# Two gated linear-attention blocks: x and A's k weights chunk by chunk over two queues, and block 2's transposing transfers over two queues

## The chip, the cores and the metric

The kernel runs on one core of a Trainium2 chip. The metric is the device time of one execution in microseconds; three executions of the kernel before are shown, and their median counts.

## The reference

One input x (2048 rows of 640, bf16) goes through two linear-attention blocks A and B, each with its own weights, and a gate mixes the two results row by row. B_x is not used.

```python
def _A_ref(x, wqkv, wo):                      # _B_ref is the same
    B, S, D = x.shape                         # 1, 2048, 640
    H = 32; Dh = D // H                       # 32 heads of 20
    qkv = ((x @ wqkv).reshape(B, S, 3, H, Dh)).transpose(2, 0, 3, 1, 4)
    q, k, v = qkv[0], qkv[1], qkv[2]
    phi = lambda t: jnp.where(t > 0, t + 1, jnp.exp(t)) + 1e-6
    pq, pk = phi(q), phi(k)
    kv = jnp.einsum("bhsd,bhse->bhde", pk, v)
    z = jnp.einsum("bhsd->bhd", pk)
    num = jnp.einsum("bhqd,bhde->bhqe", pq, kv)
    den = jnp.einsum("bhqd,bhd->bhq", pq, z)[..., None] + 1e-6
    return (num / den).transpose(0, 2, 1, 3).reshape(B, S, D) @ wo

g = sigmoid((x * gate_w).sum(-1, keepdims=True))
return g * _A_ref(x, A_wqkv, A_wo) + (1 - g) * _B_ref(x, B_wqkv, B_wo)
```

## The kernel before

The rows are cut into 16 chunks of 128 (index i) and 4 blocks of 512 (index n; block 1 holds chunks 0 to 3, block 2 chunks 4 to 7). The 640 columns are cut into 5 pieces of 128 (index c). TensorE needs x with its columns on the partitions, as the tile xT. Block 1 gets there by TensorE itself: x is loaded as it stands into xn, each chunk is transposed into PSUM (`x_transpose`, L167 to L172) and copied to xT by VectorE or ScalarE. Blocks 2 to 4 are brought by transposing transfers, one for each piece c of a block, from x in memory straight into xT (L105 to L112).

The work that the change touches lies at the start:

- L99 to L104 issue the first loads. SP's queue carries x chunks 0 and 1 in one transfer, A's k weights of pieces 1 and 3, and x chunks 2 and 3. ScalarE's queue carries A's k weights of pieces 0, 2 and 4, and the row of gate weights (`grow`), which `gate_columns` (L139) reads late in A's k stage.
- L105 to L112 issue the transposing transfers, all on SP's queue: five for block 2, then A's q weights in one transfer, then five each for blocks 3 and 4. Later loads (x for the g pass L487, A's v and output weights L437 to L445) follow on the same queue.
- L115 to L132 build masks and the identity on POOL, and L135 to L137 run eight matmuls on zeros.
- `k_first` (L197 to L210) is the first stage that reads x. It transposes chunks 0 and 1 and then runs their k matmuls with c as the outer loop, so that both chunks use each piece of the weights as it comes; chunks 2 and 3 are transposed before chunk 1's last two matmuls.
- `k_chunk` (L190 to L195) does one chunk of k: ten matmuls (two halves of 320 columns, five pieces each) into a PSUM slot, and then `k_done`, which is `phi` (L174 to L179): one exponential on ScalarE and two operations on VectorE, which write the feature map pk.

There are four PSUM slots (`ps`, L56 to L65), taken in turn; a slot is free again when `phi` or the copy has read it. After `k_first` the program runs k chunks 2 to 7 (L478), five q units of the first two blocks (L480), k chunks 8 to 15 (L482), and then the later stages: q, the sums z, the g pass (x against pk), the products with v and the output weights, then the same for B, and at last the output rows in pairs.

Nothing in this part fixes the order of the work by hand. The framework takes the program's order as a priority, may move an instruction ahead of one that is not ready by its plan, and writes each engine's instructions out in one fixed order; it also puts in every wait. Only the last stage (from L526) has an order written by hand.

Of the kernel before, what the change touches and what calls it, by code (L numbers as in the profile page):

```python
# [8 lines left out]
P = 128  # L9
FP32 = mybir.dt.float32  # L10
BF16 = mybir.dt.bfloat16
ACT = mybir.ActivationFunctionType
ALU = mybir.AluOpType

S, D, H = 2048, 640, 32
Dh = D // H
DT = D // P
ST = S // P
NB = 4
CB = 4  # L20
HB = 512
# [9 lines left out]
def kernel(  # L31
# [11 lines left out]
    nc = tc.nc  # L43
    x2 = A_x.flatten_outer_dims()
# [4 lines left out]
    wpool = ctx.enter_context(tc.tile_pool(name="wpool", bufs=1))  # L49
    work = ctx.enter_context(tc.tile_pool(name="work", bufs=2))  # L50
# [5 lines left out]
    def ps_raw(name, slot=None):  # L56

        if slot is None:
            slot = turn[0]
            turn[0] = (slot + 1) % 4  # L60
        return psum.tile([P, 4 * HB], BF16, tag=f"ps{slot}", name=name)

    def ps(name, slot=None):

        return ps_raw(name, slot).bitcast(FP32).rearrange("p (b n) -> p b n", b=2)  # L65

    xT = persist.tile([P, DT, S], BF16, name="xT")
    xn = persist.tile([P, ST, D], BF16, name="xn")
# [12 lines left out]
    zero = persist.tile([P, HB], BF16, name="zero")  # L81
    grow = persist.tile([1, D], BF16, name="grow")
# [4 lines left out]
    wq_dram = [A_wqkv.rearrange("(c p) f -> p c f", p=P), B_wqkv.rearrange("(c p) f -> p c f", p=P)]  # L87
# [6 lines left out]
    xb0 = x2[0:CB * P, :].rearrange("(p q) d -> p q d", q=CB)  # L94
    wk = [None, None]
    wv = [None, None]
    wq = [None, None]
    wk[0] = wpool.tile([P, DT, D], BF16, tag="wk", name="wkA")
    nc.sync.dma_start(out=xn[:, 0:2, :], in_=xb0[:, 0:2, :])  # L99
    for c in range(DT):  # L100
        eng = nc.sync if c % 2 else nc.scalar
        eng.dma_start(out=wk[0][:, c, :], in_=wq_dram[0][:, c, D:2 * D])
    nc.sync.dma_start(out=xn[:, 2:4, :], in_=xb0[:, 2:4, :])
    nc.scalar.dma_start(out=grow[:], in_=gate_w.rearrange("(o f) -> o f", o=1))  # L104
    for n in range(1, NB):  # L105
        if n == 2:
            wq[0] = wpool.tile([P, DT, D], BF16, tag="wq", name="wqA")
            nc.sync.dma_start(out=wq[0][:], in_=wq_dram[0][:, :, 0:D])
        for c in range(DT):
            nc.sync.dma_start_transpose(  # L110
                out=xT[:, c, n * HB:(n + 1) * HB], in_=x2[n * HB:(n + 1) * HB, c * P:(c + 1) * P]
            )  # L112


    make_identity(nc, ident[:])  # L115
# [4 lines left out]
    for sign, base in ((1, 0), (-1, Dh - 1)):  # L120
        nc.gpsimd.affine_select(
            out=maskE[:], in_=maskE[:], pattern=[[sign * P, DT], [-sign * Dh, H]],
# [3 lines left out]
    for r in range(4):  # L126
        rows = slice(32 * r, 32 * r + 32)
        for sign, base in ((1, 0), (-1, Dh - 1)):
            nc.gpsimd.affine_select(
                out=E4[rows], in_=E4[rows], pattern=[[sign, D]],  # L130
# [2 lines left out]


    warm = ps("warm", 3)  # L135
    for k in range(8):
        nc.tensor.matmul(warm[:, 0, :], lhsT=zero[:, 0:P], rhs=zero[:], start=True, stop=True)  # L137

    def gate_columns():  # L139
# [24 lines left out]
            nc.scalar.activation(out=ge[b][:], in_=pt[:, 0, :], func=ACT.Exp, scale=(-1.0, 1.0)[b])  # L164
            nc.vector.tensor_scalar(ge[b][:], ge[b][:], 1.0, 1e30, op0=ALU.add, op1=ALU.min)

    def x_transpose(i, slot, eng):  # L167
        pt = ps_raw("xt", slot)
        for c in range(DT):
            nc.tensor.transpose(out=pt[:, c * P:(c + 1) * P], in_=xn[:, i, c * P:(c + 1) * P], identity=ident[:])  # L170
        copy = nc.scalar.copy if eng == "act" else nc.vector.tensor_copy
        copy(out=xT[:, :, i * P:(i + 1) * P], in_=pt[:, 0:D].rearrange("p (c n) -> p c n", c=DT))  # L172

    def phi(dst, src, n):  # L174

        e = work.tile([P, 2, n], BF16, tag="e", name="e", bufs=3)
        nc.scalar.activation(out=e[:], in_=src, func=ACT.Exp)  # L177
        nc.vector.tensor_scalar(e[:], e[:], 1.0, EPS, op0=ALU.min, op1=ALU.add)  # L178
        nc.vector.scalar_tensor_tensor(out=dst, in0=src, scalar=1.0 + EPS, in1=e[:], op0=ALU.add, op1=ALU.max)  # L179

    def k_mm(b, i, c, pt, hf):
        nc.tensor.matmul(  # L182
            pt[:, hf, 0:HF], lhsT=xT[:, c, i * P:(i + 1) * P], rhs=wk[b][:, c, hf * HF:(hf + 1) * HF],
            start=(c == 0), stop=(c == DT - 1),
        )

    def k_done(b, i, pt):
        phi(pk[:, i, :].rearrange("p (b n) -> p b n", b=2), pt[:, :, 0:HF], HF)

    def k_chunk(b, i):  # L190
        pt = ps(f"k{'AB'[b]}")
        for hf in range(2):
            for c in range(DT):
                k_mm(b, i, c, pt, hf)
        k_done(b, i, pt)  # L195

    def k_first():  # L197

        x_transpose(0, 0, "dve")
        x_transpose(1, 1, "act")  # L200
        pts = [ps("kA", 2 + i) for i in range(2)]
        for c in range(DT):
            for i in range(2):
                for hf in range(2):
                    k_mm(0, i, c, pts[i], hf)
                if c == DT - 1 and i == 0:
                    x_transpose(2, 0, "dve")
                    x_transpose(3, 1, "act")
        for i in range(2):
            k_done(0, i, pts[i])  # L210

    def q_unit(b, m, h):

# [260 lines left out]


    k_first()
    turn[0] = 0
    for i in range(2, ST // 2):  # L478
        k_chunk(0, i)
    for m in range(DT):  # L480
        q_unit(0, m, 0)
    for i in range(ST // 2, ST):  # L482
        if i == ST - 1:
            gate_columns()
        k_chunk(0, i)
    for n in range(1, NB):
        nc.sync.dma_start(  # L487
            out=xn[:, n * CB:(n + 1) * CB, :], in_=x2[n * HB:(n + 1) * HB, :].rearrange("(q p) d -> p q d", p=P)
# [10 lines left out]

    turn[0] = 2  # L500
    k_chunk(1, 0)
    k_chunk(1, 1)
    kvt_pass(0)
# [22 lines left out]
    with tc.manual_schedule():  # L526
# [23 lines left out]
        for i in range(1, half):  # L550
            p, after = pairs[i], pairs[i + 1] if i + 1 < half else None
# [42 lines left out]
```

## Time and profile before

| what | value |
|---|---|
| median of 3 executions | 202.93 us |
| the three executions | 202.90, 202.93 and 229.24 us |
| the profiled execution's own time | 203.25 us |
| its span, first to last instruction | 201.5 us |
| TensorE busy | 195.9 us, 97% of the span |
| VectorE busy | 140.1 us, 70% |
| ScalarE busy | 76.4 us, 38% |
| transfers, mean over the span | 71 GB/s, 14.21 MB |

The profile is of one execution. Its views give a start in us from the span's beginning, a length in us, then the engine, the line of the program, the operation and what it writes and reads; a letter q behind an engine's name (SPq, ACTq) means its queue, which issues transfers and waits. "x5" counts the instructions that a row merges. PE is TensorE, DVE VectorE, ACT ScalarE, SP SyncE. A matmul's own duration in a row is longer than its share of the time, since matmuls are pipelined; the distance between two starts is what counts. The view of waits names who waited, what for, the sum in us, how many times, and the longest.

### The profile page before, as it was taken

The numbers are of one execution on the slowest core, as the hardware profiler recorded it, in microseconds if no ns is written. First come the engines' busy times: TensorE is split into PE (matmuls) and PEld (weight loads), VectorE is DVE, ScalarE is ACT, GpSimd is POOL, SyncE is SP. The second block draws the span as 40 slices with busy tenths as digits, with TensorE's granted clock in tenths as the row PEclk, the third lists the DMA queues.
The fourth block names the chain that finished last, engine by engine and source line by source line (L and its number), as shares of the span: only waits on it lengthen the run. The fifth ranks groups of instructions, "written<-read, shape, count | busy, mean of one in ns | idle before, by whom it ended". The sixth has DMA issues, their size and how long they took to land.

```text
span 201.5 us, 3645 instructions
## 1 busy us (share of the span) xinstructions
PE 195.9 (97%) x1527; PEld 123.1 (61%) x1527; DVE 140.1 (70%) x224; ACT 76.4 (38%) x105; POOL 8.5 (4%) x22
## 2 busy tenths in 40 slices
PE   7999999999999999999999999999999999999992
PEld 3676457654566667877764444566667667777761
DVE  3288679857894577677678767876578667885552
ACT  2354545454413442356552454415442531122110
POOL 8800000000000000000000000000000000000000
PEclk9999999999999999999999999999999999999999
DMA  6679479950140000140052000000000002222111
GB/s 192 183 185 155 105 214 368 190 163 3 12 152 3 0 0 3 15 148 3 0 135 53 0 0 0 5 0 0 3 0 0 3 0 87 78 79 83 65 68 65
DMA packets 18016, 14.21 MB, mean 71 GB/s; under 512 B 8736, under 2 KB 17745, under 8 KB 18001
## 3 DMA queue, kind: packets, MB, share of 16 engines
q1 hardware_dynamic: 17566, 13.50, 25.3%
q10 hardware_dynamic: 434, 0.49, 0.7%
q8 instruction: 12, 0.20, 0.4%
q14 instruction: 4, 0.02, 0.0%
HBM read 9.40 MB, written 2.62 MB: 60 GB/s over the span
## 4 chain that ended last, share of the span: by engine, by line
PE 96%; ACT 1%; DVE 1%; issue 0%; ACTq 0%
PE gB L236 11%; PE gA L236 11%; PE kA L182 11%; PE qA L218 11%; PE kB L182 11%; PE qB L218 11%; PE oy L376 5%; PE ox L376 5%; PE oz L376 5%; PE ow L376 3%; PE warm L137 2%; PE mA L300 1%; PE mid L300 1%; PE exA L352 1%; PE exB L352 1%; PE mid L279 1%
## 5 line engine op out<-in xcount | busy, mean ns | idle before, releaser
L182 PEld LDWEIGHTS <-xT 128*128 128x128 bf16 x320 | 31.0, 98 | 12.9 <-DVE xT L172 0.7
L236 PEld LDWEIGHTS <-xn 128*128 128x128 bf16 x320 | 29.8, 98 | 14.1 <-issue 2.5
L178 DVE TENSOR_SCALAR e<-e 128x640 bf16<-128x640 bf16 (+1 forms) x52 | 19.0, 366 | 18.9 <-ACT e L177 17.4
L236 PE MATMUL gB<-pk,xn 128*128 128x320 bf16 x160 | 23.3, 300 | 0.0
L236 PE MATMUL gA<-pk,xn 128*128 128x320 bf16 x160 | 23.3, 300 | 0.0
L182 PE MATMUL kA<-wkA,xT 128*128 128x320 bf16 x160 | 22.9, 302 | 0.1
L182 PE MATMUL kB<-wkB,xT 128*128 128x320 bf16 x160 | 22.9, 299 | 0.0
L218 PE MATMUL qA<-xT,wqA 128*128 128x512 bf16 x100 | 22.2, 379 | 0.0
L218 PE MATMUL qB<-xT,wqB 128*128 128x512 bf16 x100 | 22.0, 379 | 0.0
L218 PEld LDWEIGHTS <-wqB 128*128 128x128 bf16 x100 | 9.6, 98 | 11.4 <-issue 0.3
L218 PEld LDWEIGHTS <-wqA 128*128 128x128 bf16 x100 | 9.5, 97 | 11.4 <-issue 0.3
L177 ACT ACTIVATE e<-kB 128x640 bf16<-128x640 f32 x16 | 11.3, 704 | 11.7 <-PE kB L182 11.7
L177 ACT ACTIVATE e<-kA 128x640 bf16<-128x640 f32 x16 | 11.3, 705 | 11.3 <-PE kA L182 11.3
L177 ACT ACTIVATE e<-qA 128x1024 bf16<-128x1024 f32 x10 | 10.2, 1023 | 13.1 <-PE qA L218 13.1
L177 ACT ACTIVATE e<-qB 128x1024 bf16<-128x1024 f32 x10 | 10.2, 1023 | 13.1 <-PE qB L218 13.1
L179 DVE SCALAR_TENSOR_TENSOR pk<-kB,e 128x640 bf16<-128x640 f32 x16 | 13.2, 824 | 1.6
L179 DVE SCALAR_TENSOR_TENSOR pk<-kA,e 128x640 bf16<-128x640 f32 x16 | 13.2, 824 | 1.5
L179 DVE SCALAR_TENSOR_TENSOR pqTB<-qB,e 128x1024 bf16<-128x1024 f32 x10 | 12.2, 1218 | 0.9
L179 DVE SCALAR_TENSOR_TENSOR pqTA<-qA,e 128x1024 bf16<-128x1024 f32 x10 | 12.2, 1218 | 0.9
L410 ACT COPY u<-ox 128x320 f32<-128x320 f32 x8 | 3.4, 425 | 21.4 <-PE ox L376 21.4
L365 DVE TENSOR_TENSOR pqTA<-exA,pqTA 128x1024 bf16<-128x1024 f32 (+1 forms) x6 | 6.3, 1046 | 5.8 <-PE exA L352 5.8
L365 DVE TENSOR_TENSOR pqTB<-exB,pqTB 128x1024 bf16<-128x1024 f32 (+1 forms) x6 | 6.3, 1046 | 5.8 <-PE exB L352 5.8
(90 smaller groups left out, 220.6 us busy)
## 6 DMA issues: line engine op xcount, KB each, us to landing
out_dram<-osb SPq DMA_DIRECT2D x15, 160.0 KB, 1.8
xn<-in_A_x_dram SPq DMA_DIRECT2D x3, 640.0 KB, 6.0
wqA<-in_A_wqkv_dram SPq DMA_DIRECT2D x1, 800.0 KB, 5.4
wvA<-in_A_wqkv_dram SPq DMA_DIRECT2D x1, 800.0 KB, 9.8
wkB<-in_B_wqkv_dram SPq DMA_DIRECT2D x1, 800.0 KB
wqB<-in_B_wqkv_dram SPq DMA_DIRECT2D x1, 800.0 KB, 4.6
wvB<-in_B_wqkv_dram SPq DMA_DIRECT2D x1, 800.0 KB, 4.6
woA<-in_A_wo_dram SPq DMA_DIRECT2D x1, 750.0 KB, 12.2
```

The costliest lines, as they stand in the source:

```text
L137: nc.tensor.matmul(warm[:, 0, :], lhsT=zero[:, 0:P], rhs=zero[:], start=True, stop=True)
L177: nc.scalar.activation(out=e[:], in_=src, func=ACT.Exp)
L178: nc.vector.tensor_scalar(e[:], e[:], 1.0, EPS, op0=ALU.min, op1=ALU.add)
L179: nc.vector.scalar_tensor_tensor(out=dst, in0=src, scalar=1.0 + EPS, in1=e[:], op0=ALU.add, op1=ALU.max)
L182: nc.tensor.matmul(pt[:, hf, 0:HF], lhsT=xT[:, c, i * P:(i + 1) * P], rhs=wk[b][:, c, hf * HF:(hf + 1) * HF], start=(c == 0), stop=(c == D ...
L218: nc.tensor.matmul(pt[:, u, :], lhsT=wq[b][:, c, m * P:(m + 1) * P], rhs=xT[:, c, n * HB:(n + 1) * HB], start=(c == 0), stop=(c == DT - 1),)
L236: nc.tensor.matmul(pt[:, hf, 0:HF], lhsT=xn[:, i, c * P:(c + 1) * P], rhs=pk[:, i, hf * HF:(hf + 1) * HF], start=(i == 0), stop=(i == ST - 1),
L300: nc.tensor.matmul(pt[:, hf, 0:HF], lhsT=KVT[:rows, j, c * P:(c + 1) * P], rhs=wo_sb[b][:rows, j, hf * HF:(hf + 1) * HF], start=(k == 0), ...
L352: nc.tensor.matmul(pts[j // 2][:, j % 2, k * RB:(k + 1) * RB], lhsT=E4[32 * j:32 * j + 32, m * P:(m + 1) * P], rhs=rT[32 * j:32 * j + 32, ...
L365: nc.vector.tensor_tensor(out=dst, in0=src, in1=dst, op=ALU.mult)
L376: nc.tensor.matmul(dst, lhsT=left[:, c, r0:r0 + P], rhs=right[:, c, :], start=(first and c == 0), stop=(c == DT - 1), skip_group_check=not ...
L410: nc.scalar.copy(out=self.u2[:], in_=self.at("x"))
```

## The change

The first x load is cut, so that x comes as chunk 0, chunk 1, and chunks 2 and 3. These and A's five k weight pieces go out alternately on SP's and ScalarE's queues; the gate row moves to POOL's queue. Block 2's five transposing transfers are issued in the order c = 0, 3, 1, 4, 2, with 3 and 4 from ScalarE's queue and the others from SP's. A's q weights come after them on SP's queue and before block 3, as they did. A one-element exponential on ScalarE (`first`) is put between the first loads and the transposing transfers. Six matmuls on zeros run for eight.

In `k_first`, chunk 0's copy to xT is made in two parts (pieces 0 and 1, then 2 to 4), chunk 1's copy moves from ScalarE to VectorE, and the k matmuls run chunk by chunk (`k_chunk`), each half with c inside it, no longer piece by piece over both chunks. Chunks 2 and 3 are transposed between chunk 1's two halves. Nothing that is computed changes.

```diff
-    nc.sync.dma_start(out=xn[:, 0:2, :], in_=xb0[:, 0:2, :])
-    for c in range(DT):
-        eng = nc.sync if c % 2 else nc.scalar
+    def load_x(eng, lo, hi):
+        eng.dma_start(out=xn[:, lo:hi, :], in_=xb0[:, lo:hi, :])
+
+    def load_wk(eng, c):
         eng.dma_start(out=wk[0][:, c, :], in_=wq_dram[0][:, c, D:2 * D])
-    nc.sync.dma_start(out=xn[:, 2:4, :], in_=xb0[:, 2:4, :])
-    nc.scalar.dma_start(out=grow[:], in_=gate_w.rearrange("(o f) -> o f", o=1))
-    for n in range(1, NB):
-        if n == 2:
-            wq[0] = wpool.tile([P, DT, D], BF16, tag="wq", name="wqA")
-            nc.sync.dma_start(out=wq[0][:], in_=wq_dram[0][:, :, 0:D])
+
+    def load_xT(eng, n, c):
+        eng.dma_start_transpose(
+            out=xT[:, c, n * HB:(n + 1) * HB], in_=x2[n * HB:(n + 1) * HB, c * P:(c + 1) * P]
+        )
+
+    load_x(nc.sync, 0, 1)
+    load_wk(nc.scalar, 0)
+    load_wk(nc.sync, 1)
+    load_x(nc.scalar, 1, 2)
+    load_wk(nc.scalar, 2)
+    load_wk(nc.sync, 3)
+    load_wk(nc.scalar, 4)
+    load_x(nc.sync, 2, 4)
+    first = work.tile([P, 1], BF16, tag="first", name="first", bufs=1)
+    nc.scalar.activation(out=first[:], in_=zero[:, 0:1], func=ACT.Exp)
+    nc.gpsimd.dma_start(out=grow[:], in_=gate_w.rearrange("(o f) -> o f", o=1))
+    for c, eng in ((0, nc.sync), (3, nc.scalar), (1, nc.sync), (4, nc.scalar), (2, nc.sync)):
+        load_xT(eng, 1, c)
+    wq[0] = wpool.tile([P, DT, D], BF16, tag="wq", name="wqA")
+    nc.sync.dma_start(out=wq[0][:], in_=wq_dram[0][:, :, 0:D])
+    for n in range(2, NB):
         for c in range(DT):
-            nc.sync.dma_start_transpose(
-                out=xT[:, c, n * HB:(n + 1) * HB], in_=x2[n * HB:(n + 1) * HB, c * P:(c + 1) * P]
-            )
+            load_xT(nc.sync, n, c)
...
-    for k in range(8):
+    for k in range(6):
         nc.tensor.matmul(warm[:, 0, :], lhsT=zero[:, 0:P], rhs=zero[:], start=True, stop=True)
...
-    def x_transpose(i, slot, eng):
+    def x_transpose(i, slot, eng, cuts=()):
...
-        copy(out=xT[:, :, i * P:(i + 1) * P], in_=pt[:, 0:D].rearrange("p (c n) -> p c n", c=DT))
+        src = pt[:, 0:D].rearrange("p (c n) -> p c n", c=DT)
+        for lo, hi in zip((0, *cuts), (*cuts, DT)):
+            copy(out=xT[:, lo:hi, i * P:(i + 1) * P], in_=src[:, lo:hi])
...
-    def k_chunk(b, i):
-        pt = ps(f"k{'AB'[b]}")
+    def k_chunk(b, i, slot=None, between=None):
+        pt = ps(f"k{'AB'[b]}", slot)
         for hf in range(2):
             for c in range(DT):
                 k_mm(b, i, c, pt, hf)
+            if hf == 0 and between is not None:
+                between()
         k_done(b, i, pt)
 
     def k_first():
 
-        x_transpose(0, 0, "dve")
-        x_transpose(1, 1, "act")
-        pts = [ps("kA", 2 + i) for i in range(2)]
-        for c in range(DT):
-            for i in range(2):
-                for hf in range(2):
-                    k_mm(0, i, c, pts[i], hf)
-                if c == DT - 1 and i == 0:
-                    x_transpose(2, 0, "dve")
-                    x_transpose(3, 1, "act")
-        for i in range(2):
-            k_done(0, i, pts[i])
+        x_transpose(0, 0, "dve", (2,))
+        x_transpose(1, 1, "dve")
+        k_chunk(0, 0, 2)
+        k_chunk(0, 1, 3, lambda: [x_transpose(2, 0, "dve"), x_transpose(3, 1, "act")])
```

## The prediction, written before the result was known

> **What bounds the kernel now.** I read the page's busy shares first, then the chain of work that ended last in order of time, then SP's and ScalarE's timelines, the waits of SP's queue, and the answer on the line that issues the transposing transfers (L110).
>
> ```profile
> PE 195.9 (97%) x1527; PEld 123.1 (61%) x1527; DVE 140.1 (70%) x224; ACT 76.4 (38%) x105; POOL 8.5 (4%) x22
> ```
>
> TensorE is busy for 97% of the span, so an edit pays only if TensorE starts sooner, or costs if TensorE is left without data. Both can only happen in the first 20 us, where the chain reads (start, length, what):
>
> ```profile
> 1.26 3.60 PE warm L137 x8
> 4.85 0.55 PE xt L170 x5
> ...
> 5.97 2.97 PE kA L182 x18
> 8.94 0.56 PE xt L170 x10
> 9.50 0.29 PE kA L182 x2
> ...
> 9.81 8.32 PE kA L182 x60
> 18.13 10.79 PE qA L218 x50
> ```
>
> Two things are to be seen. First, from 9.81 on TensorE runs without a pause: 60 matmuls in 8.32 us, 0.136 us apart, are chunks 2 to 7, ten matmuls and 1.36 us each. Chunk 4, the first that reads block 2 (rows 512 to 1023), starts at 9.81 + 2 x 1.36 = 12.53. Second, the start runs at half pace: five transposes take 0.55 us at 4.85, ten take 0.56 us at 8.94; 18 matmuls take 2.97 us where 18 x 0.136 = 2.45 would do. The half pace ends near 6.7 us, some 5.5 us after the first matmul, although the page's clock row reads full from its first slice.
>
> ```profile
> 4.66 6.41 SPq L110 DMA_TRANSPOSE xT<-in_A_x_dram  x5
> 11.12 0.58 SPq L108 DMA_DIRECT2D wqA<-in_A_wqkv_dram  x1
> 11.75 13.91 SPq L110 DMA_TRANSPOSE xT<-in_A_x_dram  x10
> ```
>
> SP needs 6.41 us to issue block 2's five transposing transfers, 1.26 to 1.30 us each. The last is issued at about 9.82.
>
> ```profile
> L110 SPq DMA_TRANSPOSE xT<-in_A_x_dram x5: 1210/1258/1259, 4.7 to 9.8; - x5
> ...
> DMA to landing us min/median/max: 2.8/2.9/3.5
> ```
>
> From issue to landing such a transfer takes 2.8 to 3.5 us (2.7 is the least over all 15), so the last one lands at about 9.82 + 3.1 = 12.9 and chunk 4 reads it at 12.53 + 4 x 0.136 = 13.07. Block 2 is 0.2 us early: the line that this change works on has almost no slack.
>
> ```profile
> SPq L110 <- DMA wkA<-in_A_wqkv_dram: 2.0, 1, 2.0
> ```
>
> The first transposing transfer stood 2.0 us on SP's queue until a part of A's k weights had landed, data that it does not read. The program's waits are the framework's, and it makes these transfers wait for transfers of the other queue.
>
> **The change part by part.**
>
> *Loads.* x comes as chunk 0, chunk 1 and chunks 2-3; SP still issues four transfers, ScalarE four (chunk 1 in place of the gate row). At 0.39 to 0.45 us each both queues end near 2.6 as now. The first x load now carries 160 KB for 320, which landed 3.7 us after its issue at 0.8, at 4.5; the bytes to wait for halve, so I put x chunk 0 at 3.6 (between 3.3 and 4.5). The gate row moves to POOL's queue; POOL has the identity ready at 1.54, wanted at 3.8, and the row's reader is at 38.4, so nothing. Two warming matmuls fewer: 3.60 / 8 x 2 = 0.9 us, used only because x comes earlier. The one-element exponential costs below the 0.70 us of the smallest one here, on a ScalarE idle until 5.96, and takes the 1.28 us table load with it; nothing. If that cover went, each would delay ScalarE's transfers by that much.
>
> *First k chunks.* The same 20 transposes and 20 matmuls run in another order. Chunk 0's copy in two pieces is 0.49 us plus one fixed cost (0 to 0.49) on an idle VectorE; chunk 1's copy moves from ScalarE (0.69) to VectorE (0.49), behind them. TensorE could begin at 3.85 instead of 4.64, 0.8 us sooner, but at half pace, and k weights c=3 and c=4 still land near 6. Chunks 2 and 3 of x are transposed in chunk 1's middle, and VectorE may be in chunk 0's 0.40 + 0.82 us when its copy is due. Chunk 2 would start between 9.1 and 9.9, for 9.81 now: a gain of 0.7 to a loss of 0.1.
>
> *Block 2's transfers.* The order issued is c0 SP, c3 ScalarE, c1 SP, c4 ScalarE, c2 SP. The trace has no two of them on different queues. The nearest rows are the two ends: issued side by side, they go out one per 1.26 us and queue; one after the other, each costs a whole landing of 2.7 to 3.1 us. I take the second, because of the 2.0 us wait above: these transfers are held until another queue's transfer has landed. The Trainium skill, "DMA: Bandwidth & Descriptors", section "Silent corruption: two transposing streams in flight at once", speaks against the change: the transfers of two issuing engines must not be in flight together, and the later stream waits for the earlier one's full completion. No run here shows it; by that page the sum is the one below, by side-by-side issue it would be 202.6.
>
> The chain then is c0, c3, c1, c4, c2: four changes of queue. c0 queues behind x chunks 2-3, which landed at 7.2; it landed at 8.1 itself. It may be issued earlier than 4.66 now, so it lands between 6.3 (3.6 + 2.7) and 8.2; I take 7.5. Four landings of 2.9 (2.7 to 3.1, with 0.05 for the wait) are 11.6 (11.0 to 12.6). c2 lands at 19.1 (17.3 to 20.8). Chunk 4 reads c2 as its third matmul, now at 12.53 + 0.27 = 12.80. **TensorE loses 19.1 - 12.8 = 6.3 us** (4.5 to 8.0), and the front's 0.7 vanishes in that stall.
>
> What stands behind the waits. On ScalarE, c4's transfer can only go at about 13.4 and holds the queue 1.26 us: x chunk 3's copy and the exponentials of chunks 0 to 2 come after it if they are queued behind it. That moves chunk 3 to about 16, still before 19.1, so it adds nothing; VectorE then has four chunks of 1.2 us behind, less than TensorE's next 1.36 each. On SP, A's q weights and blocks 3 and 4 stand behind c2. The weights go at about 17.5 and land 5.4 us later at 22.9; the first q matmul follows c2 by 5.2 us, at 24.3. The slack is 1.4 us as now, and blocks 3 and 4 shift with TensorE. If the weights slip more, TensorE waits for them next.
>
> *The clock.* TensorE will stand nearly idle for 5 to 6 us. The trace before has no such hole; its nearest row is the start, where half pace lasted 5.5 us and so cost up to 2.7. Bounds 0 and 2.7; I take 1.0, since part of the slow phase falls on chunk 3, which has time. The Trainium skill, "TensorE: Matmul & The Clock Gate", section "What's actually happening", has the clock halved after an idle window of about 3.4 us and freed after about 3.4 busy ones; that would be an estimated 1.7 us, and a sum of 210.9.
>
> **Sum.** The profiled execution took 203.25 us (span 201.5 and 1.75 around it); 203.25 + 6.3 + 1.0 = 210.55. The median of the runs shown, 202.93, lies 0.3 lower, so I forecast **210.2 us**, with a range of its own from 207.4 (4.5 and 0) to 213.6 (8.0 and 2.7).
>
> **The rivals.**
>
> *Side by side (other side).* The two queues' transfers do not wait for each other. Place: SP and ScalarE between 3.6 and 7 us. All five are issued by about 7.5 and land by 10.5, and TensorE keeps the front's gain: 202.93 - 0.7 to + 0.1, say 202.6. It decides if c3 is issued before c0 has landed. For it: only the issue times bound block 2 now, and five per 6.41 us is what two queues would shorten. Against: the cross-queue wait in the trace.
>
> *The queues are grouped.* They wait, but SP's c0, c1, c2 go first and ScalarE's c3, c4 after them. c2 lands at 9.0, c3 goes at 9.05, c4 at 10.3 and lands at 13.1; ScalarE is free at 11.6, x chunk 3's copy (with one exponential before it) ends at 13.0, and chunk 3 starts there for 11.17 now: + 1.9, or 204.8 (204 with the copy first). For it: SP's queue ran in the program's order. Against: the program alternates, and the order has to be kept somewhere.
>
> *Later loads slip in.* While c1 waits, SP is given what is ready: A's q weights (800 KB), x for the g pass (3 x 640), A's v (800) and output weights (910). For it: the chain and the timelines show reordering by readiness (ScalarE ran an exponential at 8.98 before a copy that the program has first). At some 370 GB/s, as at 28 to 30 us, 4.5 MB take 12.3 us; c1, behind them, lands near 19.2, c2 two landings later near 25: + 12.2 and 2 for the clock, 217.1. If only the q weights and x slip in, 7.4 us of traffic end near 14.3, and it is about 211.
>
> **How the numbers follow.** One after the other 0.55, later loads 0.20, grouped 0.12, side by side 0.13. About 2% is what a measurement of this kernel can tell from no change: 198.9 to 207.0. No case gives faster by that much; 0.01. Same takes side by side, grouped and a sliver of the first: 0.25. Slower 0.74. The range from 204.5 to 217.5 leaves out side by side (0.13), the fast end of grouped (0.03) and the top of the later loads (0.03).
>
> **What would show it.** Right: SP's and ScalarE's transposing issues alternate, each about 2.9 us after the one before; a wait of SP on a DMA of xT in the waits of its queue; a hole on TensorE before chunk 4's third matmul; c2 landing near 19; transposes or matmuls at half pace after the hole. Wrong: c3 issued within 1.3 us of c0; TensorE without a hole after 9 us; q weights or x loads on SP between c0 and c1 would mean the third rival. The forecast falls if the framework does not order the two queues.

## The result and the profile after

The changed kernel takes 209.77 us (median of six executions, 207.77 to 210.41), the kernel before 203.11 us in the same rounds: a ratio of 1.032, with an interval from 1.029 to 1.035. One of the six executions of the kernel before took 229.24 us and is left out of the ratio. The profiled execution of the changed kernel took 210.41 us, the slowest of its six, with a span of 208.7, 7.2 us more than the span before.

From the page, the busy shares and the clock row:

```profile
PE 197.9 (95%) x1525; PEld 123.9 (59%) x1525; DVE 140.6 (67%) x226; ACT 75.9 (36%) x105; POOL 9.1 (4%) x23
...
PEclk9976999999999999999999999999999999999998
```

TensorE's share falls by two points, and the clock row, all nines before, has a 7 and a 6 in its third and fourth slice. A slice is 208.7 / 40 = 5.2 us, so both lie between 10 and 21 us. The chain of waits, in order of time (start, length, what), says what happened ahead of that:

```profile
0.81 3.18 DMA wkA<-in_A_wqkv_dram
4.01 1.22 SPq L106
5.28 1.25 SPq L106
6.58 2.74 DMA xT<-in_A_x_dram
9.48 1.21 ACTq L106
10.73 1.27 ACTq L106
12.05 0.71 ACT e L194
13.23 0.84 DVE pk L196
14.11 11.06 PE kA L199 x60
25.17 10.79 PE qA L229 x50
```

L106 is now the line of the transposing transfers. SP issues three of them back to back (c0, c1, c2), the last at 6.58, and that one is complete 2.74 us later, at 9.32. Only then does ScalarE issue its two (c3, c4), one behind the other at 9.48 and 10.73; the records have two waits on semaphores in its queue just ahead of them, at 9.34 and 9.40. There is no alternation. ScalarE's first exponential comes at 12.05, VectorE's feature map of chunk 0 at 13.23, and at 14.11 begin the 60 matmuls of chunks 2 to 7, which began at 9.81 before. SP's waits have the way back:

```profile
SPq L106 <- DMA xT<-in_A_x_dram: 5.6, 1, 5.6
```

SP's next transposing transfer, the first of block 3, stood 5.6 us for ScalarE's two and went at 14.12. The timelines of ScalarE, VectorE and TensorE around the hole:

```profile
9.48 2.52 ACTq L106 DMA_TRANSPOSE xT<-in_A_x_dram  x2
12.05 0.70 ACT L194 ACTIVATE e<-kA 128x640 bf16<-128x640 f32 x1 [7.84 <-issue]
12.65 0.69 ACT L189 COPY xT<-xt 128x640 bf16<-128x640 bf16 x1
12.79 0.33 DVE L195 TENSOR_SCALAR e<-e 128x640 bf16<-128x640 bf16 x1 [6.65 <-ACT e L194]
...
13.23 0.82 DVE L196 SCALAR_TENSOR_TENSOR pk<-kA,e 128x640 bf16<-128x640 f32 x1
13.97 0.48 DVE L189 COPY xT<-xt 128x640 bf16<-128x640 bf16 x1
14.11 11.06 PE L199 MATMUL kA<-wkA,xT 128*128 128x320 bf16 x60 [3.53 <-DVE pk L196]
```

ScalarE computed nothing for 7.84 us. For about the first 4.5 of them it had no work yet (the estimate is in the experiment with one transfer on ScalarE), but then chunk 0's exponential and x chunk 3's copy (L189) stood behind the two transfers in its queue. VectorE's queue has x chunk 2's copy (13.97) behind chunk 0's feature map (12.79 and 13.23), which needs that exponential. In TensorE's fixed order the first matmul after chunk 1 belongs to chunk 4, which wants the PSUM slot that chunk 0's feature map frees; chunks 3 and 2 follow it. So all of TensorE waited 3.53 us for one feature map, with its cause three engines away.

The 60 matmuls then took 11.06 us, where they took 8.32 before. The view by stretches of time shows why (busy us and count by engine, granted clock, share of the transfer engines, GB/s):

```profile
13.00:16.00 3.00, 1.89 (x8) 1.08 (x8) 2.40 (x5) 0.95 (x2) 0.00 (x0) 0.50 0.34 72
16.00:20.00 4.00, 4.00 (x18) 2.32 (x17) 1.15 (x2) 0.80 (x2) 0.00 (x0) 0.53 0.46 98
20.00:24.00 4.00, 4.00 (x32) 2.90 (x30) 2.94 (x6) 2.17 (x4) 0.00 (x0) 1.00 0.54 93
```

From 16 to 20 us TensorE is never idle, yet does 18 matmuls in 4 us, and 32 in the next 4. The clock records put half pace from 12.91 to 19.74 us. The two differences, 14.11 - 9.81 = 4.30 and 11.06 - 8.32 = 2.74, make 7.04 of the span's 7.2 us. From 25 us on the two kernels run alike.

The front did not gain either. TensorE's timeline:

```profile
3.83 0.72 PE L185 MATMUL xt<-ident,xn 128*128 128x128 bf16 x5
...
7.69 1.65 PE L199 MATMUL kA<-wkA,xT 128*128 128x320 bf16 x11 [1.24 <-DMA wkA<-in_A_wqkv_dram]
...
9.74 0.84 PE L199 MATMUL kA<-wkA,xT 128*128 128x320 bf16 x5
```

x chunk 0 landed at 3.8 us, for 4.5 before, but the last piece of A's k weights landed at 7.65 us, for 6.38 before, and chunk 0 needs all five pieces before its first half is done. Chunk 1 ends at 9.74 + 0.84 = 10.58, for 9.79 before.

### The profile page after: what moved, and what is told of

Same layout as the page of the kernel before. It is cut to its first block, busy times and chain, and to the rows that moved or that the text cites. A ratio compares the mean times of both kernels' runs of the same rounds, so it can differ in the third digit from the quotient of the medians.

```text
span 208.7 us, 3650 instructions
## 1 busy us (share of the span) xinstructions
PE 197.9 (95%) x1525; PEld 123.9 (59%) x1525; DVE 140.6 (67%) x226; ACT 75.9 (36%) x105; POOL 9.1 (4%) x23
## 2 busy tenths in 40 slices
DMA packets 18189, 14.21 MB, mean 68 GB/s; under 512 B 8782, under 2 KB 18046, under 8 KB 18174
## 4 chain that ended last, share of the span: by engine, by line
PE 90%; DMA 3%; ACTq 1%; ACT 1%; SPq 1%; DVE 1%; issue 0%; DVEq 0%
PE gB L247 11%; PE gA L247 11%; PE kA L199 11%; PE qA L229 10%; PE kB L199 10%; PE qB L229 10%; PE oy L387 5%; PE ox L387 5%; PE oz L387 5%; PE ow L387 3%; DMA wkA<-in_A_wqkv_dram 2%; DMA xT<-in_A_x_dram 1%; PE mA L311 1%; ACTq L106 1%; SPq L106 1%; PE mid L311 1%
## 5 line engine op out<-in xcount | busy, mean ns | idle before, releaser
L199 PEld LDWEIGHTS <-xT 128*128 128x128 bf16 x320 | 32.4, 102 | 19.0 <-ACT e L194 3.7
L199 PE MATMUL kA<-wkA,xT 128*128 128x320 bf16 x160 | 25.8, 325 | 4.8 <-DVE pk L196 3.5
L196 DVE SCALAR_TENSOR_TENSOR pk<-kA,e 128x640 bf16<-128x640 f32 x16 | 13.2, 825 | 1.6
L196 DVE SCALAR_TENSOR_TENSOR pk<-kB,e 128x640 bf16<-128x640 f32 x16 | 13.2, 825 | 1.6
L387 PEld LDWEIGHTS <-pqTB 128*128 128x128 bf16 x80 | 7.8, 98 | 4.1 <-issue 1.0
```

What stands on the lines that cost most here:

```text
L199: nc.tensor.matmul(pt[:, hf, 0:HF], lhsT=xT[:, c, i * P:(i + 1) * P], rhs=wk[b][:, c, hf * HF:(hf + 1) * HF], start=(c == 0), stop=(c == D ...
L387: nc.tensor.matmul(dst, lhsT=left[:, c, r0:r0 + P], rhs=right[:, c, :], start=(first and c == 0), stop=(c == DT - 1), skip_group_check=not ...
```

## The experiments

The theory was that the two queues are served in groups and not in turn, that ScalarE's wait holds back its exponentials and copies, and that the late matmuls then meet a slow clock. The rivals were that the landing of block 2 itself is what TensorE lacks, that the new front is what costs, and that it is the time for issuing the two transfers, and not the wait ahead of them, that holds ScalarE.

**All five transposing transfers on SP**, in the order c0 to c4 (the rest as changed).

```diff
-    for c, eng in ((0, nc.sync), (3, nc.scalar), (1, nc.sync), (4, nc.scalar), (2, nc.sync)):
+    for c, eng in ((0, nc.sync), (1, nc.sync), (2, nc.sync), (3, nc.sync), (4, nc.sync)):
```

> The changed kernel with all five transposing transfers of block 2 on SP, in the order c0 to c4; nothing else is undone. Theory A (ScalarE's queue: c3 and c4 wait there until SP's three have landed, the exponentials and the copy of x chunk 3 stand behind them, TensorE stands still and then runs at half pace): the hole of 3.5 us and the slow 60 matmuls both go; the first part still ends near 10.4, because the loads are as in the change, so 203.4 to 204.3 us. Rival B (block 2's data come too late): c4 lands near 12.2 by SP's 1.26 us issues, so also about 204. Rival C (the new loads and the chunk-by-chunk order are what costs): near 209.

Measured: 204.65 us, ratio 1.0077 (1.0058 to 1.0096). From the timelines of TensorE and ScalarE:

```profile
8.01 1.66 PE L199 MATMUL kA<-wkA,xT 128*128 128x320 bf16 x11 [1.00 <-DMA wkA<-in_A_wqkv_dram]
...
9.02 0.70 ACT L194 ACTIVATE e<-kA 128x640 bf16<-128x640 f32 x1 [4.82 <-PE kA L199]
...
11.48 8.32 PE L199 MATMUL kA<-wkA,xT 128*128 128x320 bf16 x60 [0.58 <-DVE pk L196]
```

Without ScalarE's transfers the 60 matmuls begin at 11.48 and run at full pace. So the queue split accounts for 14.11 - 11.48 = 2.63 us of the start and for the 2.74 of the clock: most of the loss. The time is 0.35 above the top of what the theory gave; the front alone costs 11.48 - 9.81 = 1.67 us here, with two waits for A's k weights in chunk 0 (0.71 and 1.00) and 0.58 for chunk 0's feature map.

**One transfer on ScalarE** (c4 alone, the other four on SP).

```diff
+    for c, eng in ((0, nc.sync), (1, nc.sync), (2, nc.sync), (3, nc.sync), (4, nc.scalar)):
```

> The changed kernel with only c4 on ScalarE's queue, c0 to c3 on SP. Theory A: what holds ScalarE is the wait for the other queue's landing, not the number of transfers; c3 goes at 7.9 and lands near 10.7, c4 goes then and frees ScalarE near 12.1, as late as now, so 208 to 210.5 us with the hole in place. Rival D (the two issues of 1.2 us each hold ScalarE): one issue fewer, so about 1.2 us less hole, ScalarE free near 10.8, 206 to 207.

Measured: 206.65 us, ratio 1.019 (1.0163 to 1.0216). The timelines:

```profile
9.55 1.20 ACTq L106 DMA_TRANSPOSE xT<-in_A_x_dram  x1
10.80 0.70 ACT L194 ACTIVATE e<-kA 128x640 bf16<-128x640 f32 x1 [6.60 <-PE kA L199]
...
12.86 8.32 PE L199 MATMUL kA<-wkA,xT 128*128 128x320 bf16 x60 [2.48 <-DVE pk L196]
```

The transfer still goes after SP's first three, at 9.55, but ScalarE is free 1.25 us sooner, and the 60 matmuls begin 14.11 - 12.86 = 1.25 us sooner. That is the time one transfer holds the issuing queue, and the 1.38 us that are left against 11.48 are little more than the one issue that is left (1.20); the front of this run is 0.52 us earlier than in the run before (7.49 for 8.01), which hides some of the wait. The time lies where the rival of the issue times had it (206 to 207) and below the theory's 208 to 210.5, so here the theory missed: each issue taken away gives its whole length back.

How much is the wait, and how much the issuing? With all transfers on SP the first exponential starts 1.01 us after the row of eleven matmuls (8.01 and 9.02). By that it could have started near 8.70 in the changed kernel, where the row starts at 7.69; it started at 12.05. Of these 3.35 us, an estimate, the two issues take 2.52 and the wait until 9.48 about 0.8. The wait does its harm mostly by its place: it puts the issues at the time when the exponential is due. In this run a hole of 2.48 us was followed by full pace.

**The copies of x chunks 2 and 3 taken out from behind ScalarE** (transposed between chunk 0's halves and both copied by VectorE; the transfers stay on two queues).

```diff
-        k_chunk(0, 0, 2)
-        k_chunk(0, 1, 3, lambda: [x_transpose(2, 0, "dve"), x_transpose(3, 1, "act")])
+        k_chunk(0, 0, 2, lambda: [x_transpose(2, 0, "dve"), x_transpose(3, 1, "dve")])
+        k_chunk(0, 1, 3)
```

> The changed kernel, transfers as in it, but chunks 2 and 3 of x are transposed between the halves of chunk 0 and both copied by VectorE, so that their copies do not stand behind ScalarE's queue or chunk 0's feature map. Theory A: chunks 2 and 3 run while ScalarE is held, chunk 4 waits for its PSUM slot (chunk 0's feature map, near 14.05) and for c4 (14.0), starts at 14.1 for 12.5 before the change, no half pace: 204.5 to 205.5 us. If half of the loss were elsewhere (rival C), 207 or more.

Measured: 205.03 us, ratio 1.0098 (1.0085 to 1.0111), as expected. The timelines:

```profile
8.06 0.89 DVE L189 COPY xT<-xt 128x640 bf16<-128x640 bf16 x2 [1.91 <-PE xt L185]
...
8.14 4.92 PE L199 MATMUL kA<-wkA,xT 128*128 128x320 bf16 x35
9.59 2.52 ACTq L106 DMA_TRANSPOSE xT<-in_A_x_dram  x2
12.15 1.90 ACT L194 ACTIVATE e<-kA 128x640 bf16<-128x640 f32 x3 [7.93 <-PE kA L199]
...
14.21 5.59 PE L199 MATMUL kA<-wkA,xT 128*128 128x320 bf16 x40 [1.16 <-DVE pk L196]
```

ScalarE's transfers go at the same time as in the changed kernel and its exponentials are as late, but with both copies at 8.06 TensorE has chunks 2 and 3 to work on until 13.05. The hole shrinks from 3.53 to 1.16 us, no half pace follows, and 4.7 of the 6.7 us lost come back. Chunk 4 starts at 14.21, for 12.53 before (+1.68). It waits for chunk 0's feature map, that is for ScalarE's queue again, and not for block 2 (its c3 and c4 landed at 13.71 and 14.10 here, before chunk 4 starts).

**The queue split alone, in the kernel before.**

```diff
-        for c in range(DT):
-            nc.sync.dma_start_transpose(
+        for c in (0, 3, 1, 4, 2) if n == 1 else range(DT):
+            (nc.scalar if n == 1 and c > 2 else nc.sync).dma_start_transpose(
```

> The kernel before with one thing changed: block 2's transposing transfers in the order c0, c3, c1, c4, c2 and c3 and c4 on ScalarE's queue. The instruction lists put ScalarE's two first here and let SP's three wait for them. Theory A: ScalarE issues them at 4.7 and 5.9 and is then free for its table load (1.28) and the copy of x chunk 1 only at 8.5, 2.5 us later than now; SP's c0 waits for c4's landing near 9, and c2 lands near 14.5 for 12.9; chunk 4 reads it at 14.8 for 12.8: about + 2, 204.5 to 206 us. If the transfers cost something only in the changed kernel's order of work: 203.

Measured: 205.23 us, ratio 1.0112 (1.0085 to 1.0138), as expected, but by another path:

```profile
4.76 2.52 ACTq L110 DMA_TRANSPOSE xT<-in_A_x_dram  x2
...
7.30 1.28 ACT L172 ACT_TABLE_LOAD   x1 [7.30 <-issue]
8.60 0.69 ACT L172 COPY xT<-xt 128x640 bf16<-128x640 bf16 x1
9.05 3.81 SPq L110 DMA_TRANSPOSE xT<-in_A_x_dram  x3
...
9.35 1.40 PE L182 MATMUL kA<-wkA,xT 128*128 128x320 bf16 x9 [2.31 <-ACT xT L172]
```

Here the plan put ScalarE's two first and SP's three behind them, at 9.05. What suffers is what is queued on ScalarE behind the transfers: the table load and x chunk 1's copy, which is done at 9.3; in the kernel before it began at 5.96.

**The first k stage alone** (the kernel before with the changed `x_transpose`, `k_chunk` and `k_first`, and its own loads).

```diff
-        x_transpose(0, 0, "dve")
-        x_transpose(1, 1, "act")
-        pts = [ps("kA", 2 + i) for i in range(2)]
...
+        x_transpose(0, 0, "dve", (2,))
+        x_transpose(1, 1, "dve")
+        k_chunk(0, 0, 2)
+        k_chunk(0, 1, 3, lambda: [x_transpose(2, 0, "dve"), x_transpose(3, 1, "act")])
```

> The kernel before with the changed first k chunks (copies, cuts, chunk-by-chunk matmuls) and none of the new loads or queues. It splits the 1.7 us that stay when all transposing transfers are on SP. If the order chunk by chunk costs them: 204 to 205 us. If they come from the new loads (A's last k weights land at 7.7 to 8.0 for 6.4, and chunk 0 needs all five pieces before its second half): the weights are here by 6.4, 203.0 to 203.5 us.

Measured: 203.21 us, ratio 1.0004 (0.9995 to 1.0013): the new order costs nothing with the old loads.

**The loads alone** (all five transposing transfers on SP, and the old first k stage).

```diff
-        x_transpose(0, 0, "dve", (2,))
-        x_transpose(1, 1, "dve")
-        k_chunk(0, 0, 2)
-        k_chunk(0, 1, 3, lambda: [x_transpose(2, 0, "dve"), x_transpose(3, 1, "act")])
+        x_transpose(0, 0, "dve")
+        x_transpose(1, 1, "act")
+        pts = [ps("kA", 2 + i) for i in range(2)]
...
```

> The changed loads, the one-element exponential, the gate row on POOL and six warming matmuls, all transposing transfers on SP, but the first k chunks as before (piece by piece over both chunks). If the loads alone cost the 1.7 us: 204 to 205 us. If it is late weights together with an order that needs them all for chunk 0: here only four matmuls wait for the last piece, the start is up to 0.5 us earlier than before the change, 202.4 to 203.0 us.

Measured: 202.90 us, ratio 0.9989 (0.9981 to 0.9998). TensorE's timeline after the first three k matmuls:

```profile
6.21 2.21 PE L197 MATMUL kA<-wkA,xT 128*128 128x320 bf16 x15 [0.38 <-ACT xT L187]
```

There is a short wait for a copy and none for weights. Neither half costs by itself, and together they give the ratio of 1.0077 above: with the new loads the last weight piece is late, which the old order, piece by piece over two chunks, bears and the new one doesn't.

**x chunks 0 and 1 first on both queues, x chunks 2 and 3 last** (old first k stage, transfers on SP).

```diff
...
+    load_x(nc.scalar, 1, 2)
+    load_wk(nc.sync, 0)
+    load_wk(nc.scalar, 1)
+    load_wk(nc.sync, 2)
+    load_wk(nc.scalar, 3)
+    load_wk(nc.sync, 4)
+    load_x(nc.scalar, 2, 4)
...
```

> As the run with the changed loads alone, but x chunks 0 and 1 go first on the two queues, the weights alternate behind them with the last piece on SP ahead of the transposing transfers, and x chunks 2 and 3 are last on ScalarE's queue. If the last weight piece's landing is what holds the start: it lands near 6.2, and the kernel beats the one before, 202.0 to 202.8 us. If the half pace of the first 6.7 us sets the start whatever the loads do: 202.7 to 203.2.

Measured: 202.68 us, ratio 0.9979 (0.9969 to 0.999). This is the lowest median of all versions, 0.2% below the kernel before. Its interval overlaps those of the run above and of the next one, so the three are not told apart. The reason given for a gain did not hold: the last weight piece landed at 7.57 us, not near 6.2, while the k matmuls start at 5.17, for 5.97 in the kernel before.

**The same with x chunks 2 and 3 last on SP.**

```diff
-    load_x(nc.scalar, 2, 4)
+    load_x(nc.sync, 2, 4)
```

> As the run with x chunks 0 and 1 first, but x chunks 2 and 3 follow the last weight piece on SP, so that nothing but one queue's tail shares with it; transposing transfers all on SP, k piece by piece over both chunks. If the last piece's landing (7.6 to 7.8 in the last two runs) sets the end of the start, it lands near 6 and the kernel gains another 0.3 us: 202.1 to 202.6. If not: 202.6 to 202.9 as in that run.

Measured: 202.85 us, ratio 0.9983 (0.9972 to 0.9994). Not the further gain that was expected, though the last weight piece landed sooner, at 6.95; its first k matmuls begin at 5.12 (5.17 in the version before), and the start's half pace lasts until 5.6 us.

**These loads with the new order of the first k stage** (the transposing transfers all on SP).

```diff
-    load_wk(nc.scalar, 0)
-    load_wk(nc.sync, 1)
     load_x(nc.scalar, 1, 2)
-    load_wk(nc.scalar, 2)
-    load_wk(nc.sync, 3)
-    load_wk(nc.scalar, 4)
+    load_wk(nc.sync, 0)
+    load_wk(nc.scalar, 1)
+    load_wk(nc.sync, 2)
+    load_wk(nc.scalar, 3)
+    load_wk(nc.sync, 4)
...
```

> The loads of the run before this one with the changed k chunk by chunk. If the 1.6 us that the new loads and the chunk order cost together (and neither alone) come from weights that are late where chunk 0 needs all five, they are gone here: 202.1 to 203.2 us. If they come from the order of the copies and of chunk 4's first matmul behind chunk 0's feature map: 203.8 to 204.7.

Measured: 203.54 us, ratio 1.0047 (1.0026 to 1.0067), between the two expectations. TensorE's timeline:

```profile
6.32 1.65 PE L199 MATMUL kA<-wkA,xT 128*128 128x320 bf16 x11 [0.26 <-DMA wkA<-in_A_wqkv_dram]
...
9.91 7.37 PE L199 MATMUL kA<-wkA,xT 128*128 128x320 bf16 x53 [0.71 <-DVE pk L196]
```

The wait for weights falls from 1.71 us in all (0.71 and 1.00 in the first experiment) to 0.26, and the matmuls of chunks 2 to 7 begin at 9.91, for 11.48. So, by the profiled executions, 1.57 of the front's 1.67 us was late weights. The 0.71 us for chunk 0's feature map stays: with x chunk 2's copy and chunk 4's first matmul both behind it, that order leaves a hole even when the loads are early.

**Two attempts to keep TensorE busy through the hole.** The first put 16 matmuls on zeros after chunk 1, into the unused half of x chunk 3's slot.

```diff
...
+        spare = pts[1].bitcast(FP32).rearrange("p (b n) -> p b n", b=2)[:, 1, :]
+        for k in range(16):
+            nc.tensor.matmul(spare, lhsT=zero[:, 0:P], rhs=zero[:], start=True, stop=True)
```

> The changed kernel with 16 matmuls on zeros of 512 columns put behind chunk 1, in the hole, into the unused second bank of the slot of x chunk 3's transposes. They leave every other wait as it is. Theory A with the clock as a second term: the chunks still begin near 14.1, 4.3 us later than before the change, but 60 matmuls take 8.3 us for 11.1, so 206.8 to 207.5 us. If the slow matmuls come from something else than the idle hole: unchanged at 209 to 210.

Measured: 211.97 us, ratio 1.0437 (1.0405 to 1.047). The plan put the fillers behind the hole and not into it:

```profile
14.09 0.30 PE L200 MATMUL kA<-wkA,xT 128*128 128x320 bf16 x1 [3.46 <-DVE pk L197]
...
14.22 2.97 PE L226 MATMUL xt<-zero 128*128 128x512 bf16 x12
```

So the fillers only added their own time, and the run does not answer its question. It shows one thing by accident: its hole was 3.46 us, almost that of the changed kernel, and in its profile the granted clock stayed at 1.00 from 13 to 24 us. Two of its four executions had a mean clock of 1.00 and took 211.06 and 211.16 us; the two at .989 and .992 took 212.78 and 212.80.

The second put 30 smaller ones into unused columns of chunk 1's own slot, so that they had to run before its feature map.

```diff
+        if slot == 3:
+            for k in range(30):
+                nc.tensor.matmul(pt[:, 1, HF:HB], lhsT=zero[:, 0:P], rhs=zero[:, 0:HB - HF], start=True, stop=True)
```

> The changed kernel with 30 matmuls on zeros of 192 columns behind chunk 1's last matmul, into unused columns of its own PSUM slot, which wait for nothing; the earlier filling stood behind a wait and lengthened the work instead. They end near 12.9, inside the hole. If the half pace comes from the idle hole: chunks 2 to 7 still begin 4.3 to 4.7 us later than before the change but run at full pace in every run, 207.2 to 207.8 us, and the runs spread less than the changed kernel's 207.8 to 210.4. If the slow matmuls have another cause: 209 to 210 with the same spread.

Measured: 208.25 us, ratio 1.0275 (1.025 to 1.0299), above what was expected. From the timelines of TensorE and VectorE:

```profile
11.04 1.27 PE L185 MATMUL xt<-ident,xn 128*128 128x128 bf16 x10
...
13.33 2.64 PE L216 MATMUL kA<-zero 128*128 128x192 bf16 x30
...
13.83 0.82 DVE L196 SCALAR_TENSOR_TENSOR pk<-kA,e 128x640 bf16<-128x640 f32 x1
...
15.80 8.31 PE L199 MATMUL kA<-wkA,xT 128*128 128x320 bf16 x60
```

The hole is filled and the 60 matmuls run at full pace, 8.31 us. But in this execution, at 209.32 us one of the two slowest of five, the half pace of the start lasted until 13.2 us (ten transposes took 1.27 us at 11.04, for 0.72 in the changed kernel at 9.18), and the 60 matmuls began 1.69 us later than in the changed kernel. Chunk 0's feature map accounts for 0.60 of that (it starts at 13.83, for 13.23); the other 1.1 us are the fillers' own, since they end after the feature map does. The clock's share is therefore shown by the changed kernel's own records, and only in part by this run.

## Why the prediction was right, and where it was wrong

The time was right within 0.5 us, and that was luck: it did not come by the way that the prediction took. The prediction had a stall of 6.3 us and 1.0 for the clock; in the profiled execution the 60 matmuls began 4.30 us late and lost 2.74 to the clock. Its forecast was the sequence "one after the other"; the one that came was the rival "the queues are grouped", at a price three and a half times what was put on it: 209.77 - 203.11 = 6.66 us for 1.9.

**Right.** Transfers of two queues do not overlap: c3 went at 9.48, 0.16 us after c2's landing at 9.32, and SP's next at 14.12, 0.08 after c4's at 14.04. The Trainium skill, "DMA: Bandwidth & Descriptors", section "Silent corruption: two transposing streams in flight at once", asks for just that, and both changes of queue in this trace agree with it. There was a hole on TensorE before chunk 4, and half pace after it. But the hole stood before chunk 4's first matmul, which wanted a PSUM slot, and not before its third, for c2.

The row on which the prediction built the wait does not show it. In the instruction records of the kernel before, the first transposing transfer (4.66) waits on the same semaphore that it will itself count up when it lands. The k weight piece that landed at 4.65 had used that semaphore before it, so the 2.0 us were a wait for a semaphore to come free, and the same wait stands ahead of the first transposing transfer in the changed kernel (1.4 us). The waits that keep the two queues apart are others, those at 9.34 and 9.40 on ScalarE's queue.

**Wrong: the order.** The step that failed is "The chain then is c0, c3, c1, c4, c2: four changes of queue." The plan made two groups and two changes, SP to ScalarE and back. Block 2 was complete at 14.04, not at 19.1. The program's alternation was not kept; when ScalarE was given one transfer it went after three of SP's, and in the kernel before with the same split ScalarE's two went first. The prediction gave the grouping 0.12, and put against it that the program alternates and that the order has to be kept somewhere.

**Wrong: where the loss is.** "That moves chunk 3 to about 16, still before 19.1, so it adds nothing" was said of the work behind ScalarE's transfers. That work was the path. The experiment with both copies on VectorE leaves the transfers where they are and brings back 4.7 us.

**Wrong: the price of the grouped rival.** It counted x chunk 3's copy alone (chunk 3 at 13.0). It missed that VectorE's x chunk 2 copy stood behind chunk 0's feature map, and that TensorE's order has chunk 4's first matmul, which wants that feature map too, ahead of chunks 3 and 2. So the exponential at 12.05 held all three, and the start was 14.11. It also gave the clock nothing.

**Mis-sized: the front.** It was put between a gain of 0.7 and a loss of 0.1, on the sentence that the weights "still land near 6". They landed at 7.65, chunk 1 ended 0.79 us later than before, and with all transfers on SP the 60 matmuls began 1.67 later. The loads and the order cost nothing apart (202.90 and 203.21 us) and give 204.65 together. In the changed kernel x chunks 2 and 3 (320 KB) are issued at 2.19 us, beside the last weights; with them issued last, at 2.67, TensorE's wait for weights is 0.26 us. That version also moves all five weight pieces to the other queue and issues x chunk 1 ahead of them, so the issue of x chunks 2 and 3 alone was not told apart.

**Mis-sized: the clock.** Taken 1.0 with bounds 0 and 2.7; the profile has 2.74. The six executions carry it: their mean granted clock was .997 in the one of 207.77 us, .992 in that of 209.17, .989 at 209.38, and .980 or .981 in the three of 210.16 to 210.41. In the profile, .981 is the 6.83 us at 0.50 and 1.2 us more at the end of the span; by the same sum .992 and .989 stand for some 3.3 and 4.6 us at half pace, and .997 for 1.2. So part of the change's cost is a slow phase that comes at differing lengths, and the spread of 2.6 us is nearly all of it.

The sum of the changed kernel, by the profiled executions: front +1.67, ScalarE's queue +2.63, clock +2.74, together 7.04 of 7.2 us. The first two terms come from the run with all transfers on SP, whose front was slightly later than the changed kernel's own (chunk 1 ended at 10.90, not 10.58), so their border is good to about 0.3 us.

What stays open: what decides in the plan which queue's group goes first, and whether a hole's length or its place in time decides the slow phase (the last section has what speaks for the place). Transfers on ScalarE queued behind its exponentials were not run.

## What to carry to other kernels

A second queue for transfers that may not overlap is no second lane: count the changes of queue, and at each one the wait for the other queue's landing and the issue time, and then read what is queued behind the waiting instruction on a compute engine, down to its last reader. When two parts of a change cost nothing alone, run them together before believing it: here the order of the loads and the order that uses them cost 0.8% only in company. And a number that comes out right proves no step; here only the trace showed that another sequence had made it.

## What the runs showed of the hardware

- A transposing transfer of 512 x 128 holds ScalarE's queue 1.20 to 1.27 us, as it does SP's (1.22 and 1.25 us in the chain above). On ScalarE this is time in which no exponential ran.
- The granted clock fell to 0.50 for one stretch of 6.83 us, from 12.91 to 19.74, after TensorE had idled from 10.58. Holes of 3.46 and 2.48 us in two other kernels were followed by a clock of 1.00. A hole of about 3.5 us cost nothing in one profile and 2.74 us in the other.
- In all thirteen profiles the time between two changes of the granted clock is a whole multiple of 3.413 us: 6.83, 6.83 and 187.73 us in the changed kernel (2, 2 and 55 times), 194.56 in the kernel before (57 times). In the stretch of 3.41 us that ended when the clock fell, at 12.91, TensorE had worked 1.08 us. The hole of 3.46 us lay across two such stretches, with 2.0 and 1.4 us of work in them, and the clock stayed. So the place of a hole on this grid may decide; two profiles do not prove it.
- The half pace of the start ended between 4.6 and 6.7 us in twelve of the profiled executions, and at 13.2 in one. The Trainium skill, "TensorE: Matmul & The Clock Gate", section "What's actually happening", explains such scatter by a window that runs freely, beside the kernel; that nearly the same hole gave both outcomes here agrees with it, and the 6.83 us are about two of its windows of 3.4. The page puts the scatter of the start at 0.5 us either way; it was larger here.
